# The first keys at the head of the DMA queue, with their last 2 KB columns in eight transfers of 8 rows

## The chip, the core and the metric

The kernel runs on one core of a Trainium2 chip. A core has five engines that run their own instruction streams and meet only at semaphores: TensorE (PE, matrix products; its weight loads are listed as PEld), VectorE (DVE), ScalarE (ACT), GpSimd (POOL) and SyncE (SP). Data come from HBM by DMA transfers. Here all of them are issued from SP's queue, one after the other, and carried by 16 DMA engines that work side by side. The metric is device time in microseconds, the median of several runs; a profiled execution gives the trace behind the views that are quoted.

## What is computed

One decode step, for four sequences of one token each, through two layers of the same weights: attention over a long cache of keys and values, then a gated feed-forward block, and both again.

```python
B, Sq, D = 4, 1, 512
Hq, Hkv, Sk, Dh = 32, 8, 8192, 128

def _A_ref(x, k_cache, v_cache, wq, wo):
    q = (x @ wq).reshape(B, Sq, Hq, Dh).transpose(0, 2, 1, 3)
    k = jnp.repeat(k_cache, rep, axis=1)
    v = jnp.repeat(v_cache, rep, axis=1)
    p = _softmax(jnp.einsum("bhqd,bhkd->bhqk", q, k) * (Dh ** -0.5))
    o = jnp.einsum("bhqk,bhkd->bhqd", p, v)
    return o.transpose(0, 2, 1, 3).reshape(B, Sq, Hq * Dh) @ wo

def _B_ref(x, w_gate, w_up, w_down):
    return (_silu(x @ w_gate) * (x @ w_up)) @ w_down

x = x + _A_ref(_layernorm(x), k_cache, v_cache, wq, wo)
x = x + _B_ref(_layernorm(x), w_gate, w_up, w_down)
x = x + _A_ref(_layernorm(x), k_cache, v_cache, wq, wo)
x = x + _B_ref(_layernorm(x), w_gate, w_up, w_down)
```

All inputs are bf16. The two caches are 67 MB each and both layers read both, so nearly all of the kernel's bytes are keys and values.

## The kernel before

**Tiles.** A unit `u` is one batch entry with a pair of key-value heads; there are 16 (`NP`). The keys of a unit are one tile of 128 rows by 32 KB (4 MB), and so are its values: row `p` holds 128 consecutive positions (`TT`) of one head, rows 0 to 63 the first head of the pair, rows 64 to 127 the second. Tiles lie in a ring of four slots of SBUF (`kv[:, s, :]`, `s` 0 to 3; a fifth slot, `QS`, holds `wq` at first). A slot is counted in eight parts (`NB`) of 4 KB columns (`BW` = 2048 elements); the set `free` and the resource names `s0.3` and so on go by such parts.

**What is done with a tile.** VectorE turns the keys in place, in blocks of 32 by 32 (`turn`, L484 with the instruction on L488): part by part for the first unit of a layer, two parts at once for most others. TensorE multiplies each part with the placed queries `zq` (`scores`, L505 with L512: four products of 128 x 512 per part). Then come the maximum, the exponentials (ScalarE, L559), the turned probabilities (L576) and the products with the values (L644). When a part of a tile is used up, `finished` calls `freed`, and that calls `pump`.

**What sets the order of the transfers.** The list `cmds` (L347 to L365) holds every load in the order in which SP issues it: the first keys `K(0, us[0])`, the second keys, the first values, then the other keys and values in turn, with the four pieces of `wo` inserted, the feed-forward weights behind them, and layer 1. A function per entry (`half`, `twos`, `ends`) cuts a tile into several transfers of fewer columns. `pump` (L406) issues entries from the front of the list for as long as the parts that they fill are free, and stops at the first that isn't. SP issues in that order and never out of it; a transfer whose slot is still being read waits on SP for the reader's semaphore, and everything behind it waits too. `load` (L425) issues one entry. A load of a whole tile counts on its slot's semaphore, a part of one on a semaphore of its own (`part_sem`).

**The start.** Lines L926 to L929 issue `wq`'s first half (2 MB), the token rows `A_x` (4 rows of 1 KB, into `xio`), `wq`'s second half, and then call `pump`, which issues keys 0, keys 1, values 0, `wo` piece 0 and keys 2; the next entry, values 1, needs slot 0 and stops it. TensorE transposes the token rows (L932), `center` (L807) takes the mean off, `qproj` (L834) makes the queries with `wq` (two passes of 64 products each, L841, the deviation in between, L827 to L831) and places them (L502). Only then does the loop over the units begin, with the turns of keys 0.

**The end.** The last transfers are layer 1's last values, the gate and up weights, and the down weights in three pieces (`wd0`, `wd1`, `wd2`; 608.21, 608.69 and 632.87 us). The last products (L903) wait for each piece in turn; their sums are copied (L965, L967) and stored.

Of the kernel before, what the change touches and what calls it, by code (L numbers as in the profile page):

```python
# [103 lines left out]
def bass_interleave_layers__gqa_block_cached__swiglu_ffn__decode_kernel(  # L104
# [18 lines left out]
    P = 128  # L123
# [6 lines left out]
    NB = 8  # L130
# [7 lines left out]
    QH = NB // NH  # L138
    assert 2 * QH * REP == QB and QH * Dh == 512
    ZP = QB - REP  # L140
    NSLOT = 4
# [3 lines left out]
    with ExitStack() as es:  # L145
        sb = lambda name, shape, dt: es.enter_context(nc.sbuf_tensor(name, shape, dt))

        SL = TT * Dh
        BW = TB * Dh
# [6 lines left out]
        kv = kvf[:, 0:(NSLOT + 1) * SL].rearrange("p (s w) -> p s w", s=NSLOT + 1)  # L156
# [63 lines left out]
        n = FO * B  # L220
# [8 lines left out]
        xio = pb[0:B, 0:D]  # L229
        acc2 = pbf[:, Dh:2 * Dh]  # L230
        row = acc2[0:B]
        PB = ["pb", "gr", "eg", "gw", "hT", "xs", "vs", "lnv", "xx", "xc", "row"]
# [39 lines left out]
        sem_x = sem("sem_x")  # L272
# [5 lines left out]
        def part_sem():  # L278
            n_part[0] += 1
            return sem(f"sem_p{n_part[0]}")  # L280

        es.enter_context(nc.Block())
        T = _Sync(engines, prog)
# [6 lines left out]
             reads=["ident"], writes=["ident"])  # L290
        T.op("pool", lambda e: e.memset(quad[:], 0.0), writes=["quad"])
        for a in range(NA):
# [11 lines left out]
             reads=["ident"], writes=["head"])  # L304
# [3 lines left out]
             reads=["ident"], writes=["made"])  # L308
        T.op("dve", lambda e: e.tensor_reduce(sel[:].rearrange("p (h r) -> p h r", h=2),
                                              made.rearrange("p (h q r) -> p h r q", h=2, q=QH), AX.X, ALU.max),  # L310
             reads=["made"], writes=["sel"])
        T.op("dve", lambda e: e.tensor_reduce(own[:], made.rearrange("p (h q r) -> p q h r", h=2, q=QH),
                                              AX.XY, ALU.max),
             reads=["made"], writes=["own"])
# [7 lines left out]
        order = [list(range(NP)), [NP - 1, NP - 2, NP - 3, NP - 4] + list(range(NP - 4))]  # L322
        turn_of = {}

        K = lambda L, u: ("K", L, u)
# [10 lines left out]
        ends = lambda it, s: [(it, s, 0, QH), (it, s, QH, NB - 1), (it, s, NB - 1, NB)]  # L336
# [3 lines left out]
        def placed(seq, ring, parts):  # L340
            out = []
            for i, it in enumerate(seq):
                s = ring[i % len(ring)]
                out += parts[i](it, s) if i in parts else [(it, s, 0, NB)]
            return out
# [1 line left out]
        us = order[0]  # L347
        seq = [K(0, us[0])] + loads(0, 1)
        assert len(seq) == 2 * NP
        cmds = placed(seq, (0, 1, 2, 3), {len(seq) - 1: ends})  # L350
        where = {it: s for it, s, _, _ in cmds}
        assert [where[it] for it in (K(0, NP - 1), V(0, NP - 2), V(0, NP - 1))] == [0, 2, 3]
        for n, i in ((3, 0), (6, 1), (9, 2), (12, 3)):
            cmds.insert(n, (("wo", i), None, 0, 0))
        cmds += [(("W", 0), W_SLOT[0], 0, NB), (("W+", 0), W_SLOT[0], NB, NB + 1)]

# [14 lines left out]
        def load_weight(name, i=0, s=0):  # L371
            if name == "wq":
                n = 2 * HqDh
                T.dma("sp", kv[:, QS, i * n:(i + 1) * n],
                      A_wq[i * 2 * P:(i + 1) * 2 * P, :].rearrange("(p e) f -> p (e f)", e=2), sem_w["wq"][i],
                      writes=[f"wq{i}"])
            elif name == "wo":
                src = A_wo[i * H2 * Dh:(i + 1) * H2 * Dh, :]
                T.dma("sp", wo_sb[:, i * H2:(i + 1) * H2, :].rearrange("p (c j) n -> p c (j n)", j=NA),
                      src.rearrange("(c p j) n -> p c (j n)", p=P, j=NA), sem_w["wo"][i], writes=[f"wo{i}"])  # L380
            else:
                w0 = kvf[:, s * SL:(s + 1) * SL]
                if name == "W+":
                    load_wd(w0, i, NW - 1, ["late"])
                    return
                T._wait("pool", T._need((), [f"s{s}.{NB - 1}"]))
                T.op("pool", lambda e: e.memset(late_pT(s).bitcast(FP32), 0.0), writes=["late"])
                T.dma("sp", w0[:, 0:KT * F].rearrange("p (c x) -> p c x", c=2),
                      B_w_gate.rearrange("(c p e) f -> p c (e f)", c=2, e=2), sem_w["wg"][0],
                      writes=[f"s{s}.{q}" for q in range(NB)] + ["wg"])  # L390
                up = B_w_up.rearrange("(c p e) f -> c p (e f)", c=2, e=2)
                if i == 0:
                    T.dma("sp", wres[:, 0:2 * F], up[0], sem_w["wu"][0], writes=["wu0"])
                    T.dma("sp", wres[:, 2 * F:], up[1, :, 0:FY], sem_w["wu"][1], writes=["wu1"])
                T.dma("sp", w0[:, O_WU:O_WD], up[1, :, FY:], sem_w["wu"][2], writes=["wu2"])

                for j in range(NW - 1):
                    load_wd(w0, i, j)
# [4 lines left out]
                  B_w_down[a * P:b * P, :].rearrange("(m p e) n -> p m (e n)", p=P, e=e_), sem_w["wd"][j],  # L403
                  writes=[f"wd{j}"] + list(also))

        def pump():  # L406
            while issued[0] < len(cmds):
                it, s, a, b = cmds[issued[0]]
                if it[0] == "wo":
                    load_weight(*it)  # L410
                else:
                    need = {(s, q) for q in range(a, b)}
                    if not need <= free:
                        return
                    free.difference_update(need)
                    if it[0] in ("W", "W+"):
                        load_weight(it[0], it[1], s)
                    else:
                        slot_of[it] = s
                        load(it, a, b, sem_s[s] if b - a == NB else part_sem())  # L420
                issued[0] += 1

        q_gone = set()

        def load(it, a, b, sm):  # L425
            kind, L, u = it
            s = slot_of[it]
            gp, bt = pair_gb(u)
            src = (A_k_cache if kind == "K" else A_v_cache)[bt, 2 * gp:2 * gp + 2, :, :].rearrange(
                "h (p t) d -> (h p) (t d)", t=TT)  # L430
            over = [w for i, w in enumerate(WQ) if s == QS and a // (NB // 2) == i and w not in q_gone]
            q_gone.update(over)
            T.dma("sp", kv[:, s, a * BW:b * BW], src[:, a * BW:b * BW], sm,
                  writes=[f"s{s}.{q}" for q in range(a, b)] + over)

        def freed(s, a, b):
            free.update((s, q) for q in range(a, b))
# [46 lines left out]
        def turn(L, u, q, n):  # L484
            s = slot_of[K(L, u)]
            w = kv[:, s, q * BW:(q + n) * BW].bitcast(FP32)
            names = [f"s{s}.{i}" for i in range(q, q + n)]
            T.op("dve", lambda e: e.transpose(w, w), reads=names, writes=names)  # L488
            turned.update((L, u, i) for i in range(q, q + n))
# [317 lines left out]
        def center(between=lambda: None):  # L807
            T.op("dve", lambda e: e.tensor_reduce(xs, xT[:].rearrange("p (k b) -> p b k", b=B), AX.X, ALU.add),
                 reads=["x"], writes=["xs", "pb", "row"])
            at, name = place("ln", 0, B)  # L810
            T.op("pe", lambda e: e.matmul(at, lhsT=ones, rhs=xs, start=True, stop=True),
                 reads=["xs", "onesf"], writes=[name])
            between()
            total = at.unsqueeze(1).to_broadcast([P, KT, B])
            T.op("dve", lambda e: e.scalar_tensor_tensor(bk3(xn[:]), total, -1.0 / D, bk3(xT[:]),
                                                         op0=ALU.mult, op1=ALU.add),
                 reads=["x", name], writes=["xn"])
            T.op("dve", lambda e: e.scalar_tensor_tensor(bk3(xc), total, -1.0 / D, bk3(xT[:]),
                                                         op0=ALU.mult, op1=ALU.add),
                 reads=["x", name], writes=["xc"])  # L820
            T.op("dve", lambda e: e.tensor_tensor(xx, xc, xc, ALU.mult), reads=["xc"], writes=["xx"])
            T.op("dve", lambda e: e.tensor_reduce(vs, xx.rearrange("p (k b) -> p b k", b=B), AX.X, ALU.add),
                 reads=["xx"], writes=["vs"])
# [99 lines left out]
            add_to_x(bank(k)[:, 0:XB], f"pb{k}")  # L923


        load_weight("wq", 0)  # L926
        T.dma("sp", xio, A_x.rearrange("b s d -> (b s) d"), sem_x, writes=PB)
        load_weight("wq", 1)
        pump()  # L929
        xb = bank_bf(OUTB)  # L930
        for kt in range(KT):
            T.op("pe", lambda e: e.matmul(xb[:, kt * B:(kt + 1) * B], lhsT=xio[:, pick2(kt)],  # L932
# [3 lines left out]
        for L in range(2):  # L936
            us = order[L]
            turn_of.update((u, i % 2) for i, u in enumerate(us))
            totals.clear()
            mixed.clear()  # L940
            center()
            qproj(L, us[0])
            if L:
                for q in (NB - 2, NB - 1):
                    hold(q, True)
                freed(QS, NB // 2, NB - 2)
            todo = [("K", 0)]
            for i in range(1, NP - 1):
                todo += [("K", i), ("V", i - 1)]
            todo[-1:] = [("K", NP - 1)] + [("V", i) for i in range(NP - 3, NP)]  # L950
            for kind, i in todo:
                if kind == "V":
                    values(L, us[i])
                    continue
                keys(L, us[i], us[min(i - 1, NP - 3)] if i else None, AHEAD if L and i == 1 else LAG)
            drain(0.0)
            flush()
            center(lambda: x_rows(0) if L else None)
            ffn(L)
# [39 lines left out]
```

## Time and profile before

| What | Value |
|---|---|
| Median of 3 runs | 647.24 us (647.04 to 647.56) |
| The profiled execution: its own time | 647.04 us |
| Its span, first to last recorded instruction | 645.2 us (1.8 us of its time lie outside) |
| Granted TensorE clock, mean | 0.83 |
| Busy: PE, PEld, DVE, ACT, POOL | 419.2, 181.6, 422.1, 41.2, 11.1 us |
| Bytes read from HBM | 272.9 MB, 423 GB/s over the span |
| First key turn of VectorE (L488) | 24.37 us |
| First product of scores (L512) | 25.67 us |
| Slot 0 free, values 1 issued by SP | 35.11 us |
| Output issued by SP | 643.61 us |

Busy times are sums over the span; an engine that is idle two fifths of the time in the mean can still be the one waited for in a stage. The clock of the profile runs in microseconds from the span's start, and "granted clock" is the share of full speed that TensorE was allowed.

Beside the instructions, the trace has a record for each DMA packet (start, duration, size, queue) and for each step of each DMA semaphore. A transfer of 128 rows raises its semaphore in 16 steps, one when each DMA engine has landed its share. The packets carry no engine's number, but each engine's packets follow one another without a gap, so that the time of the 16 steps shows how the engines stand against each other.

### The profile page before, as it was taken

The page shows a single profiled execution, that of the slowest core. Times are in us where ns is not written, and L with a number is a line of the kernel's source. Part 1 is how long each engine was busy: PE and PEld are TensorE (multiplying, and loading weights), DVE is VectorE, ACT ScalarE, POOL GpSimd, SP SyncE. Part 2 cuts the span into 40 slices and gives each one's busy share as a digit, 9 for nine tenths or more (in the row PEclk, how much of TensorE's full clock was granted, in tenths as well). Part 3 has the DMA queues.
Part 4 walks back from the last instruction along what each step waited for, and adds up shares of the span by engine and source line. Part 5 has one row for each costly group of instructions (what it writes and reads, how often), then busy time and mean ns, then how long its engine had stood idle before and what let it go on. Part 6 is the DMA issues. An engine that isn't in the chain of part 4 may idle for free.

```text
span 645.2 us, 7417 instructions
## 1 busy us (share of the span) xinstructions
PE 419.2 (65%) x3128; PEld 181.6 (28%) x3128; DVE 422.1 (65%) x595; ACT 41.2 (6%) x117; POOL 11.1 (2%) x43
## 2 busy tenths in 40 slices
PE   3483475456765756757867877777555676557877
PEld 2121122122222312322226432233222222222325
DVE  1585467456776556776962778878655577665964
ACT  1000000000000000000010010000000000000110
POOL 0000000000000000000000000000000000000000
PEclk9995887688876888777975899997768987679787
DMA  9999999999999999999999999999999999999997
GB/s 366 442 425 416 441 430 431 424 429 438 433 425 432 439 424 430 431 439 426 427 414 410 421 440 430 427 432 434 427 428 439 428 431 427 440 427 428 433 416 276
DMA packets 14560, 273.36 MB, mean 424 GB/s; under 512 B 1464, under 2 KB 1472, under 8 KB 5312
## 3 DMA queue, kind: packets, MB, share of 16 engines
q1 hardware_dynamic: 14528, 272.91, 99.2%
q8 instruction: 24, 0.39, 0.2%
q14 instruction: 8, 0.07, 0.0%
HBM read 272.90 MB, written 0.00 MB: 423 GB/s over the span
## 4 chain that ended last, share of the span: by engine, by line
DMA 62%; DVE 20%; PE 13%; issue 3%; another core or an unknown queue 1%; SPq 0%; ACTq 0%; ACT 0%; DVEq 0%
DMA kvf<-in_A_k_cache_dram 50%; DVE kvf L488 16%; DMA kvf<-in_A_v_cache_dram 11%; PE ps L512 8%; PE ps L644 2%; DMA kvf<-in_B_w_down_dram 2%; DVE pb L694 1%; PE ps L841 1%; PE ps L882 0%; DVE pb L690 0%; DVE kvf L453 0%; DVE scr L704 0%; SPq L93 0%; PE ps L523 0%
## 5 line engine op out<-in xcount | busy, mean ns | idle before, releaser
L512 PE MATMUL ps<-kvf,zq 128*128 128x512 bf16 x1024 | 296.1, 436 | 191.9 <-DVE kvf L488 188.2
L488 DVE STREAM_TRANSPOSE kvf<-kvf 128x2048 f32<-128x2048 f32 (+1 forms) x135 | 280.3, 2102 | 127.9 <-DMA kvf<-in_A_k_cache_dram 127.8
L512 PEld LDWEIGHTS ps<-kvf,zq 128*128 128x128 bf16 x1024 | 100.3, 109 | 349.9 <-DVE kvf L488 230.2
L644 PE MATMUL ps<-kvf,pT 128*32 128x512 bf16 x960 | 65.8, 396 | 1.4 <-DVE pT L576 1.4
L559 ACT ACTIVATE pb<-ps,tiny 128x512 bf16<-128x512 f32 x32 | 22.0, 688 | 537.3 <-DVE tiny L557 500.7
L576 DVE STREAM_TRANSPOSE pT<-pb 64x512 bf16<-64x512 bf16 x60 | 41.2, 687 | 3.6 <-ACT pb L559 2.6
L694 DVE SCALAR_TENSOR_TENSOR pb<-ps,tiny,pb 128x128 f32<-128x128 f32 x104 | 36.5, 351 | 4.4 <-PE ps L644 0.7
L518 DVE TENSOR_REDUCE tiny<-ps 128x1 f32<-128x512 f32 x32 | 22.0, 687 | 21.4 <-PE ps L512 21.4
L644 PEld LDWEIGHTS ps<-kvf,pT 128*32 128x32 bf16 x960 | 20.8, 98 | 31.0 <-issue 15.3
L699 PEld LDWEIGHTS ps<-sel,pb 128*128 128x128 f32 x64 | 16.8, 271 | 16.4 <-DVE pb L694 7.9
L502 POOL TENSOR_TENSOR zq<-scr,tiny 128x64 bf16<-128x64 bf16 x30 | 9.0, 299 | 563.3 <-PE ps L512 563.3
L526 DVE TENSOR_REDUCE mrm<-ps 1x8 f32<-1x128 f32 x32 | 8.8, 274 | 13.8 <-PE ps L523 13.8
L549 PEld LDWEIGHTS ps<-mrm,tiny 128*128 128x128 f32 x60 | 13.4, 229 | 9.4 <-DVE scr L704 3.2
L699 PE MATMUL ps<-sel,pb 128*128 128x8 f32 x64 | 12.4, 267 | 5.3 <-DVE pb L694 5.3
L549 PE MATMUL ps<-mrm,tiny 128*128 128x16 f32 x60 | 10.2, 248 | 3.1 <-ACT mrm L561 3.1
L690 DVE TENSOR_SCALAR pb<-ps,tiny 128x128 f32<-128x128 f32 x32 | 10.1, 316 | 2.6 <-PE ps L644 2.6
L760 PE MATMUL ps<-wo_sb,scr 128*4 128x512 bf16 x48 | 11.0, 379 | 0.6 <-DVE scr L729 0.6
L523 PE MATMUL ps<-identf,tiny 128*1 128x128 f32 x32 | 8.6, 270 | 1.8 <-DVE tiny L518 1.8
L561 ACT ACTIVATE mrm<-head,tiny 128x8 f32<-128x8 f32 x32 | 9.6, 300 | 1.0
L841 PE MATMUL ps<-xn,kvf 128*128 128x4 bf16 x256 | 7.4, 166 | 1.9 <-DMA kvf<-in_A_wq_dram 1.1
L882 PE MATMUL ps<-xn,kvf 128*128 128x4 bf16 x224 | 7.2, 169 | 1.6 <-DMA kvf<-in_B_w_up_dram 1.2
L841 PEld LDWEIGHTS ps<-xn,kvf 128*128 128x128 bf16 x256 | 7.3, 105 | 2.1 <-DMA kvf<-in_A_wq_dram 1.2
(83 smaller groups left out, 113.7 us busy)
## 6 DMA issues: line engine op xcount, KB each, us to landing
kvf<-in_A_k_cache_dram SPq DMA_DIRECT2D x28, 4096.0 KB, 31.0
kvf<-in_A_v_cache_dram SPq DMA_DIRECT2D x27, 4096.0 KB, 35.2
kvf<-in_A_v_cache_dram SPq DMA_DIRECT2D x4, 2048.0 KB, 18.4
kvf<-in_A_k_cache_dram SPq DMA_DIRECT2D x7, 1024.0 KB, 9.8
kvf<-in_A_wq_dram SPq DMA_DIRECT2D x2, 2048.0 KB, 10.1
wo_sb<-in_A_wo_dram SPq DMA_DIRECT2D x4, 1024.0 KB, 41.3
kvf<-in_B_w_gate_dram SPq DMA_DIRECT2D x2, 1792.0 KB, 23.6
kvf<-in_A_v_cache_dram SPq DMA_DIRECT2D x2, 1536.0 KB, 34.1
```

Of the source, the lines that this page charges most:

```text
L488: T.op("dve", lambda e: e.transpose(w, w), reads=names, writes=names)
L512: T.op("pe", lambda e: e.matmul(bank(bk)[:, 0:SW], lhsT=zq[:, z0:z0 + P], rhs=w[:, :, c // 2, :, c % 2], start=(q == 0 and c == 0), stop=( ...
L518: T.op("dve", lambda e: e.tensor_reduce(mx[:], bank(bk)[:, 0:SW], AX.X, ALU.max), reads=[f"pb{bk}"], writes=["mx"])
L549: T.op("pe", lambda e: e.matmul(at, lhsT=ones, rhs=mrm[:, i * H2:(i + 2) * H2], start=True, stop=True), reads=[f"m8{i}", "rsm", "onesf"], ...
L559: T.op("act", lambda e: e.activation(pb[:], bank(bk)[:, 0:SW], ACTF.Exp, bias=nm, accum_out=rs), reads=[f"pb{bk}", "nm"], writes=PB + ["rs"])
L576: T.op("dve", lambda e: e.transpose(dst, pb[hp]), reads=["pb", "row"], writes=[name])
L644: T.op("pe", lambda e: e.matmul(bank(k)[j * QB:(j + 1) * QB, q0 * Dh:q1 * Dh], lhsT=p_t[:, t, h, :], rhs=v[:, q0:q1, t, :], start=((last o ...
L690: T.op("dve", lambda e: e.tensor_scalar(into, o, own[:, q:q + 1], None, op0=ALU.mult), reads=[f"pb{k}", "own"], writes=["row"] if last els ...
L694: T.op("dve", lambda e: e.scalar_tensor_tensor(into, o, own[:, q:q + 1], into, op0=ALU.mult, op1=ALU.add), reads=[f"pb{k}", "own", iname], ...
L699: T.op("pe", lambda e: e.matmul(at, lhsT=into, rhs=sel[:], start=True, stop=True), reads=[iname, "sel"], writes=[name])
L760: T.op("pe", lambda e: e.matmul(bank(OUTB)[0:B, 0:D], lhsT=oT[:, h, :], rhs=wo_sb[:, h, :], start=(gp == groups[L][0] and r == 0), stop=(g ...
L841: T.op("pe", lambda e: e.matmul(at[:, h * B:(h + 1) * B], lhsT=wq_sb[:, kt, h * Dh:(h + 1) * Dh], rhs=xn[:, kt * B:(kt + 1) * B], start=(k ...
```

## The change

```diff
-        cmds = placed(seq, (0, 1, 2, 3), {len(seq) - 1: ends})
+        cmds = placed(seq, (0, 1, 2, 3), {0: half, len(seq) - 1: ends})
...
-        for n, i in ((3, 0), (6, 1), (9, 2), (12, 3)):
+        for n, i in ((4, 0), (7, 1), (10, 2), (13, 3)):
...
-        def pump():
-            while issued[0] < len(cmds):
+        def pump(most=len(cmds)):
+            while issued[0] < most:
...
+        LOW, H, BESIDE = BW // 2, P // 2, NSLOT - 1
+        low_unit = K(0, order[0][0])
+
+        def raised():
+            s, c = slot_of[low_unit], SL - LOW
+            U16 = mybir.dt.uint16
+            T.op("dve", lambda e: e.tensor_copy(kv[H:P, s, c:SL].bitcast(U16), kv[0:H, BESIDE, c:SL].bitcast(U16)),
+                 reads=["low"], writes=[f"s{s}.{NB - 1}", f"s{BESIDE}.{NB - 1}"])
...
-            T.dma("sp", kv[:, s, a * BW:b * BW], src[:, a * BW:b * BW], sm,
-                  writes=[f"s{s}.{q}" for q in range(a, b)] + over)
+            names = [f"s{s}.{q}" for q in range(a, b)]
+            c = b * BW - LOW if (it, b) == (low_unit, NB) else b * BW
+            T.dma("sp", kv[:, s, a * BW:c], src[:, a * BW:c], sm, writes=names + over)
+            if c < b * BW:
+                both = src[:, c:SL].rearrange("(h p) w -> p h w", h=2)
+                sm = part_sem()
+                for j in range(NB):
+                    T.dma("sp", kv[j:H:NB, s:BESIDE + 1:BESIDE - s, c:SL], both[j:H:NB], sm,
+                          writes=["low"] if j == NB - 1 else [])
...
+        pump(1)
+        T.dma("sp", xio, A_x.rearrange("b s d -> (b s) d"), sem_x, writes=PB)
+        pump(2)
         load_weight("wq", 0)
-        T.dma("sp", xio, A_x.rearrange("b s d -> (b s) d"), sem_x, writes=PB)
         load_weight("wq", 1)
-        pump()
+        pump(5)
...
             center()
+            if not L:
+                for q in range(0, NB, 2):
+                    if q == QH:
+                        raised()
+                        pump()
+                    turn(L, us[0], q, 2)
             qproj(L, us[0])
```

In SP's queue the order is now: the first half of keys 0 (128 rows by 16 KB), the token rows, the second half without its last 2 KB (128 by 14 KB), eight small transfers, `wq` in two halves, keys 1, values 0 and `wo` piece 0. Each small transfer `j` takes the last 2 KB of rows j, j+8, ... j+56 of both heads: 8 partitions by two places by 2 KB, 32 KB in all. The first head's rows land where they belong in slot 0, the second head's land in partitions 0 to 63 of slot 3, which is still empty. `raised` copies these from slot 3 to partitions 64 to 127 of slot 0, and keys 2, which go to slot 3, wait on SP for that copy. The four turns of keys 0, two parts each, now stand on VectorE ahead of `qproj`, with the copy between the second and the third; TensorE's order of products is as before.

## The prediction

> **What bounds the kernel now.** I first read the slices of the span and the DMA queues on the profile's page.
>
> ```profile
> DMA  9999999999999999999999999999999999999997
> GB/s 366 442 425 416 441 430 431 424 429 438 433 425 432 439 424 430 431 439 426 427 414 410 421 440 430 427 432 434 427 428 439 428 431 427 440 427 428 433 416 276
> ...
> q1 hardware_dynamic: 14528, 272.91, 99.2%
> q8 instruction: 24, 0.39, 0.2%
> q14 instruction: 8, 0.07, 0.0%
> ```
>
> The 16 DMA engines work from the first slice to the last but one. The time is theirs, unless a stage hides a pause. The table of windows asks that stage by stage (columns: stretch and its length, busy us and instructions of PE, PEld, DVE, ACT, POOL, then clock, DMA share, GB/s):
>
> ```profile
> 2.00:17.00 15.00, 5.40 (x152) 4.92 (x152) 2.37 (x12) 0.58 (x3) 0.10 (x1) 1.00 0.97 406
> 17.00:50.00 33.00, 19.67 (x100) 7.28 (x100) 21.18 (x21) 1.08 (x3) 0.60 (x2) 1.00 1.00 428
> 50.00:300.00 250.00, 150.48 (x888) 60.23 (x888) 158.76 (x198) 14.02 (x40) 3.59 (x12) 0.79 1.01 431
> ```
>
> No pause: the share stays at 1, while PE and DVE work 150 and 159 of 250 us. The chain of waits and the totals of waits seem to say otherwise:
>
> ```profile
> DMA kvf<-in_A_k_cache_dram 50%; DVE kvf L488 16%; DMA kvf<-in_A_v_cache_dram 11%; PE ps L512 8%; PE ps L644 2%; DMA kvf<-in_B_w_down_dram 2%; DVE pb L694 1%; PE ps L841 1%; PE ps L882 0%; DVE pb L690 0%; DVE kvf L453 0%; DVE scr L704 0%; SPq L93 0%; PE ps L523 0%
> ...
> DVE kvf L488 <- DMA kvf<-in_A_k_cache_dram: 127.8, 24, 8.8
> ```
>
> The chain walks from a turn back to the issue of its keys and from there to the product that freed the slot, so turns get 16%. But a key tile lands 31.0 us after its issue (median on the page) and takes 9.7 to carry: some 20 us of it is queueing behind earlier tiles. DVE waits for the DMA, not the reverse. The end, in the timeline:
>
> ```profile
> 641.12 1.80 PE L903 MATMUL ps<-kvf,pb 128*4 128x128 bf16 x56
> 642.53 0.10 PEld L903 LDWEIGHTS ps<-kvf,pb 128*4 128x4 bf16 x8 [0.25 <-DMA kvf<-in_B_w_down_dram]
> 642.94 0.59 DVE L967 CAST pb<-ps 4x128 bf16<-4x128 f32 x2 [1.88 <-PE ps L903]
> 643.61 0.29 SPq L969 DMA_DIRECT2D out_dram<-pb  x1
> ```
>
> The last products wait for the last piece of the down weights; 2.7 us later (645.2 - 642.49) all is over. So the question is what sets 642.49, and the answer is in the trace's semaphore records. For three transfers: when the first of the 16 DMA engines had landed its share, and how much later the others had (us).
>
> ```
> keys 0          22.50  0.00 0.05 0.07 0.09 0.10 0.12 0.13 0.14 0.16 0.21 0.22 0.23 0.41 0.51 0.90 1.85
> values, L0     285.28  0.00 0.03 0.04 0.13 0.38 0.47 0.90 1.55 1.56 1.59 1.61 1.62 1.63 1.70 1.82 2.13
> down, piece 2  638.31  0.00 0.06 0.14 0.38 0.54 0.76 0.81 2.51 3.66 3.69 3.71 3.79 3.86 3.89 3.96 4.18
> ```
>
> DMA engines fall behind one at a time, in jumps of about 1.45. The packet records show why: at 18.81 the first of the 24 instruction packets of 16 KB (q8) sits in one engine's stream and takes 1.0 us, and the key packet behind it takes some 0.45 longer than its neighbours; 48.95, 87.47, 128.17 repeat it. 24 packets on 8 engines are 3 each, 4.3 us; at the end eight engines are 2.5 to 4.2 behind and eight within 0.81. The second eight carry no such packets, have idled a little between the layers (about 352 to 362 us), and wait for nobody. **The end is that of the eight late DMA engines, which never pause.**
>
> **The change part by part.**
>
> *Bytes between DMA engines.* A transfer of 128 rows gives each engine 8 rows. The token load of 4 rows shows in the packets as one 1 KB row on each of four engines, none on the other twelve. By that row I take an 8-row transfer to use eight engines, the same eight in all eight transfers. The other eight lose 8 rows x 2 KB. A key tile advances an engine by 9.715 us (landings, 275.57 to 285.28) for 8 rows of 32 KB, so 2 KB are 0.0759 and the eight rows 0.607. Keys 0 now also come in two pieces; a halved tile advances 4.90 per half (618.13 to 623.03), not 4.86: +0.045 for one more transfer. Lighter eight: 0.045 - 0.607 = **-0.56**. Heavier eight: 16 packets of 2 KB, 0.080 from start to start in the last down weights, 1.28, plus 0.006 to 0.045 for each of eight transfers, less 0.607, plus 0.045: +0.77 to +1.08, and I take +0.9.
>
> [...]
>
> *Which eight are late?* The engine hit at 18.81 is none of the four that carried the tokens (followed packet by packet from 7.5 us). Later hits can't be told apart, since streams then coincide within 1 ns. If the token engines belong to the eight that get the small transfers, this speaks for the late ones being the other eight. I take that: -0.56 at the end.
>
> *SP.* Nine more issues at about 0.4 us (0.38 and 0.36 in the timeline) make some 4 us. They lie beside 10 us of queued keys. Without that cover they would cost 4 us.
>
> *wq, moved behind keys 0.* In before `wq` has landed at 13.68; now 4 MB later, about 23.4 to 24.5. From its landing to placed queries is 3.0 us (13.68 to 16.68): first products at 26.4 to 27.5, not 25.67. The turns, 4 x 2.30 = 9.2 for 8 x 1.14, then lie between 11 and 20, when DVE idled 7.4 us; the copy (64 rows of 1024 16-bit elements) between 0.4 (the 128x256 cast) and 0.7 (the 64x512 transpose), taken as 0.7, fits there too. Then 32 products at 0.24 (8 in 1.91 us) or at the mean row's 0.436 are 7.6 to 14 us: slot 0 free at 34.0 to 41.5, not 35.11. Values 1 are issued up to 6 us later, but keys 2 keep the queue busy to 54.2. The second keys, freed at 45.9, slip to 52 at most, with work queued to 66. PE catches up after 50 (150 of 250 us). Cost 0; it would cost only beyond some 13 us.
>
> *The new wait on SP.* Keys 2 wait for the copy, near 15 to 17 us; behind them stand values 1 and all else. DMA has `wq`, keys 1, values 0 and `wo` until 44.5 us. Cost 0; without that cover, the delay of the copy.
>
> *The tail* follows the last landing unchanged. Sum, against the profiled execution: span 645.2 - 0.56 = 644.6, its time 647.04 - 0.56 = 646.5. The median lies 0.2 above that execution, 647.24, which gives **646.7 us**.
>
> **Rivals.**
>
> *The heavier eight are the late ones.* Then the end moves by +0.77 to +1.08: 648.0 to 648.3. For it: only one hit could be placed. Against: that one.
>
> *Each small transfer costs its whole landing.* The output store of 4 KB, alone in the queue, lands 1.27 us after its issue (643.61 to 644.88). If eight in a row each held their engines so long, 10.2 us replace 0.61; less the 3.4 by which the latest of the eight leads at the end and the 0.65 of pause it could skip, 5.5 us remain: 652.8, slower. It decides from 0.58 us a transfer. Against: consecutive transfers in the queue add 0.045, and landing is paid beside the next ones. [...]
>
> *The early keys bring the pipeline forward.* If the chain of waits were the bound, the end would follow slot 0: at best from 35.11 to 34.0, -1.1, and -0.56 more from the relieved engines: -1.7, 645.6, faster by 0.26%. For it: the chain. Against: queueing of 20 us behind every issue.
>
> *It does nothing that shows.* If the small transfers spread over all 16 engines, only the cost of more packets stays: +0.05 to +0.3, 647.3 to 647.5. Against: the token load's four packets.
>
> **How the numbers follow.** Forecast 0.60; early keys 0.15; no shift 0.10; heavier eight late 0.10; whole landings 0.05. About 0.2% (1.3 us) is what a measurement of this kernel can tell from no change. The forecast is -0.09%: within. Of its 0.60 and the rivals near zero, 0.66 stay within; faster 0.21 (the early keys and fetches that fall better than here); slower 0.13 (whole landings, and a heavier eight that pays more than the row of 0.080 says). The forecast's own range is 646.2 to 647.0; the range with the cases that are left, 645.5 to 648.3.
>
> **What would show it.** The landings of keys 0 should have two groups, eight engines about 1.4 us behind the other eight; at the last down weights eight engines should still be last, by some 2 us instead of 3.6, and the last step should come near 641.9. First turns near 11 us, first products near 27, values 1 issued between 34 and 41.5, and DMA at 1.00 in the windows to 300 us. Wrong if the last step comes later than 642.5, if the eight small transfers take over 4.6 us on their engines, or if the DMA share drops before 60 us.

## The result: 648.64 us, 1.45 us slower

| | Median | Range | Runs |
|---|---|---|---|
| Before, in the same measurements | 647.19 us | 646.86 to 647.56 | 11 |
| With the change | 648.64 us | 648.36 to 649.69 | 11 |

The ratio is 1.0023, with a 95% interval of [1.0015, 1.0031]: slower. The middle of the interval lies a little above the 0.2% that the prediction took for the least that can be told here, its lower end a little below. The time is outside the predicted range of 646.2 to 647.0, and outside 645.5 to 648.3, the range with the other cases. The profiled execution took 648.36 us, its span 646.6 us; before it was 647.04 and 645.2.

**The slices and the queues of the changed kernel** look much as before:

```profile
DMA  8999999999999999999999999999999999999996
GB/s 342 448 426 417 425 443 430 422 427 443 426 422 443 430 423 435 438 424 431 436 406 410 421 433 435 436 423 429 442 421 432 435 430 432 429 434 429 430 415 262
...
q8 instruction: 24, 0.39, 0.2%
q14 instruction: 8, 0.07, 0.0%
```

No slice shows a pause. **The windows of the changed kernel** (columns as before: PE, PEld, DVE, ACT, POOL busy, then clock, DMA share, GB/s) do show something:

```profile
12.00:14.00 2.00, 0.00 (x0) 0.00 (x0) 2.00 (x2) 0.00 (x0) 0.00 (x0) 1.00 1.12 294
14.00:17.00 3.00, 0.00 (x0) 0.00 (x0) 2.73 (x3) 0.00 (x0) 0.00 (x0) 1.00 1.00 426
17.00:22.00 5.00, 2.30 (x66) 2.21 (x66) 2.74 (x2) 0.19 (x1) 0.00 (x0) 1.00 0.99 423
22.00:50.00 28.00, 21.87 (x180) 9.33 (x180) 13.01 (x15) 1.45 (x5) 0.60 (x2) 1.00 1.01 430
50.00:300.00 250.00, 150.19 (x888) 60.20 (x888) 157.62 (x198) 14.03 (x40) 3.59 (x12) 0.80 1.00 430
```

From 12 to 14 us, while the eight small transfers are carried, the DMA engines are recorded as busy all the time and move 294 GB/s instead of some 430. The busy share of 1.12 shows nothing of it; the last column does. Over two microseconds this column scatters: the same stretch reads 557 in the kernel before, and 401 and 483 in the first two kernels of the experiments, in which nothing is held up. 294 lies below all of these, and the durations of the packets, further down, are the firmer evidence. The stretches after it move 423 to 430 GB/s.

**The timeline of the start**, changed kernel (start, duration, engine, line, operation):

```profile
1.61 5.55 SPq L93 DMA_DIRECT2D kvf<-in_A_k_cache_dram  x9
7.20 0.92 SPq L93 DMA_DIRECT2D kvf<-in_A_wq_dram  x2
...
10.04 4.49 DVE L504 STREAM_TRANSPOSE kvf<-kvf 128x2048 f32<-128x2048 f32 x2
14.78 0.42 DVE L431 COPY kvf<-kvf 64x1024 uint16<-64x1024 uint16 x1 [0.24 <-DMA kvf<-in_A_k_cache_dram]
15.23 0.34 SPq L93 DMA_DIRECT2D kvf<-in_A_k_cache_dram  x1
15.23 4.50 DVE L504 STREAM_TRANSPOSE kvf<-kvf 128x2048 f32<-128x2048 f32 x2
...
27.40 3.17 PE L528 MATMUL ps<-kvf,zq 128*128 128x512 bf16 x7 [0.35 <-DVE zq L518]
```

The reordered work does what the forecast said: `wq` is issued while 7 us of queued transfers are still being carried, the turns begin at 10.04, the copy takes 0.42 and releases keys 2 on SP at once, the scores begin at 27.40. Values 1 are issued at 36.77 (35.11 before), keys 3 at 46.33 (45.90): the pipeline has caught up.

**The timeline of the end**, changed kernel:

```profile
642.51 1.80 PE L919 MATMUL ps<-kvf,pb 128*4 128x128 bf16 x56
643.92 0.10 PEld L919 LDWEIGHTS ps<-kvf,pb 128*4 128x4 bf16 x8 [0.26 <-DMA kvf<-in_B_w_down_dram]
644.34 0.60 DVE L991 CAST pb<-ps 4x128 bf16<-4x128 f32 x2 [1.88 <-PE ps L919]
645.01 0.30 SPq L993 DMA_DIRECT2D out_dram<-pb  x1
```

The weights wait for the last down weights as before, only later: their last step came at 643.88 instead of 642.49, +1.39, and the 2.7 us behind it are the same. The loss is all in the landings. Here are the semaphore steps of the changed kernel in the form of the prediction's table (first engine, and how much later the others):

```
keys 0, second half     11.97  0.00 0.03 0.05 0.07 0.12 0.13 0.18 0.23 0.24 0.31 0.32 0.33 0.34 0.34 0.36 0.59
wq, first half          17.86  0.00 0.02 0.04 0.09 0.14 0.14 0.15 0.17 1.29 1.31 1.31 1.48 1.49 1.51 1.57 1.57
down, piece 2, layer 0 347.63  0.00 0.01 1.11 1.31 1.43 1.45 1.51 1.59 1.84 1.89 2.69 2.85 2.91 2.92 3.07 4.22
down, piece 2, layer 1 639.24  0.00 0.12 0.15 0.53 0.57 0.80 1.18 1.73 2.96 2.97 3.03 3.12 3.14 4.33 4.45 4.64
```

The two groups of eight are there after the small transfers. But half of `wq` advances an engine by 4.90, and the lighter eight took 17.86 - 11.97 = 5.89: they were late by 0.99, where they should have been on time. The packet records say why. The 2 KB packets take 0.084 us until 12.0, then up to 0.178 (mean of all 128: 0.116). `wq`'s 16 KB packets on the other engines take 0.95 to 1.05 us between 12 and 13.5, and 0.611 to 0.626 from 14.5 on.

### The profile page after: what moved, and what is told of

It is laid out like the page before. It is cut to its first block, busy times and chain, and to the rows that moved or that the text cites. A ratio compares the mean times of both kernels' runs of the same rounds, so it can differ in the third digit from the quotient of the medians.

```text
span 646.6 us, 7422 instructions
## 1 busy us (share of the span) xinstructions
PE 414.7 (64%) x3126; PEld 179.1 (28%) x3128; DVE 422.0 (65%) x592; ACT 41.2 (6%) x117; POOL 11.1 (2%) x43
## 4 chain that ended last, share of the span: by engine, by line
DMA 60%; DVE 20%; PE 14%; issue 3%; SPq 1%; ACT 0%; ACTq 0%; DVEq 0%
DMA kvf<-in_A_k_cache_dram 45%; DVE kvf L504 16%; DMA kvf<-in_A_v_cache_dram 11%; PE ps L528 9%; DMA kvf<-in_A_wq_dram 3%; DMA kvf<-in_B_w_down_dram 2%; PE ps L660 2%; DVE pb L710 2%; SPq L93 1%; PE ps L857 1%; DVE pb L706 0%; PE ps L898 0%; DVE ps L472 0%; DVE kvf L469 0%; PE ps L539 0%
## 5 line engine op out<-in xcount | busy, mean ns | idle before, releaser
L528 PE MATMUL ps<-kvf,zq 128*128 128x512 bf16 x1024 | 292.6, 431 | 185.8 <-DVE kvf L504 180.8
L528 PEld LDWEIGHTS ps<-kvf,zq 128*128 128x128 bf16 x1024 | 99.0, 108 | 342.8 <-DVE kvf L504 225.1
L715 PEld LDWEIGHTS ps<-sel,pb 128*128 128x128 f32 x64 | 16.5, 266 | 16.0 <-DVE pb L710 7.8
```

What stands on the lines that cost most here:

```text
L528: T.op("pe", lambda e: e.matmul(bank(bk)[:, 0:SW], lhsT=zq[:, z0:z0 + P], rhs=w[:, :, c // 2, :, c % 2], start=(q == 0 and c == 0), stop=( ...
L715: T.op("pe", lambda e: e.matmul(at, lhsT=into, rhs=sel[:], start=True, stop=True), reads=[iname, "sel"], writes=[name])
```

## The experiments

The edits are against the changed kernel, those of the two ladders against the kernel before; `...` marks lines left out. "Latest" is the last of 16 steps of a transfer.

### The order alone, and one transfer in place of eight

```diff
-            c = b * BW - LOW if (it, b) == (low_unit, NB) else b * BW
+            c = b * BW
...
-                        raised()
```

> Keys 0 go first in two whole halves (128 rows by 16 KB), their turns stand ahead of the queries, and there are no small transfers and no copy. Theory A (the loss is made by the eight small transfers: they weigh on DMA engines that turn out to be late, and slow the others while they run): 646.9 to 647.3, no change; wq's first half lands 4.9 us after keys 0's second half on every DMA engine, and at wq's second half the 16 steps lie as before, within 0.9 of each other, not in two groups. Rival B (the new order itself costs, by a later start of the products or the wait of later loads): 648.2 to 648.7, with the small transfers adding nothing.

Measured: 647.01 us, ratio 0.9998 [0.9989, 1.0007]. `wq`'s first half comes 4.90 behind keys 0 on all 16 engines. From 12 us on (windows of the kernel with the order alone):

```profile
12.00:14.00 2.00, 0.00 (x0) 0.00 (x0) 2.00 (x2) 0.00 (x0) 0.00 (x0) 1.00 0.94 401
14.00:17.00 3.00, 0.00 (x0) 0.00 (x0) 3.00 (x3) 0.00 (x0) 0.00 (x0) 1.00 1.02 437
```

The early keys, the early turns and the late `wq` cost nothing and bring nothing that the interval of 0.1% to either side could show. This kernel is the base of the comparisons below.

```diff
-                for j in range(NB):
-                    T.dma("sp", kv[j:H:NB, s:BESIDE + 1:BESIDE - s, c:SL], both[j:H:NB], sm,
-                          writes=["low"] if j == NB - 1 else [])
+                T.dma("sp", kv[:, s, c:SL], src[:, c:SL], part_sem(), writes=["low"])
```

> The last 2 KB columns of keys 0 come by one transfer of 128 rows instead of eight of 8 rows, with no copy; order as in the changed kernel. Theory A (uneven load): every DMA engine carries 8 packets of 2 KB, no two groups; if only the uneven load and not the 2 KB pieces are at fault, packets of 0.08 to 0.09 us and 647.0 to 647.4. Theory C (2 KB reads 32 KB apart crowd the same part of memory, whoever makes them): packets of 0.15 us or more, every engine 0.5 to 0.8 later at wq's first half, and 647.7 to 648.1 in the end.

```profile
12.00:14.00 2.00, 0.00 (x0) 0.00 (x0) 2.00 (x2) 0.00 (x0) 0.00 (x0) 1.00 1.15 483
```

Measured: 647.01 us, ratio 0.9995 [0.9986, 1.0004]. All 128 packets of 2 KB took 0.084, `wq`'s beside them 0.611. (In place of the copy, VectorE waits for the transfer.) Packets of 2 KB are not the cause.

### Is it where the eight transfers read?

Their rows lie 256 KB apart in HBM (8 rows of 32 KB). Here each reads 32 KB that lie together, so that the last 8 positions of each row of keys 0 are other data.

```diff
-                    T.dma("sp", kv[j:H:NB, s:BESIDE + 1:BESIDE - s, c:SL], both[j:H:NB], sm,
+                    T.dma("sp", kv[j:H:NB, s:BESIDE + 1:BESIDE - s, c:SL],
+                          src[j].rearrange("(p h w) -> p h w", p=NB, h=2), sm,
```

> The eight small transfers keep their shape and destination but each reads one stretch of 32 KB without gaps, so the last 2 KB columns of the first keys hold other data. Theory C (rows 256 KB apart slow the memory): packets of 2 KB back at 0.08 us, wq's 16 KB packets beside them at 0.61, wq's first half 4.9 us behind keys 0 on the eight lighter engines, heavier ones still 1.3 to 1.5 behind these; end 0.5 to 0.9 earlier than the changed kernel, 647.7 to 648.1, still slower than before, since heavier engines are among the late ones. Rival D (eight engines with small packets slow the rest whatever they read): packets at 0.16, 5.9 us, and 648.6 as in the changed kernel.

```profile
12.00:14.00 2.00, 0.00 (x0) 0.00 (x0) 2.00 (x2) 0.00 (x0) 0.00 (x0) 1.00 1.15 303
```

Measured: 648.74 us, ratio 1.0025 [1.0016, 1.0035], as the changed kernel; 2 KB packets up to 0.179, `wq`'s 0.94 to 1.05. It isn't the reads.

### A ladder of transfers, first a failed marking

Meant to mark the DMA engines by giving each another load: transfers of 1, 2, ... 15 neighbouring rows of 4 KB behind keys 0 of the kernel before, with all of `wo` moved ahead of values 0.

```diff
+        for r in range(1, NA * KT):
+            s, o = 2 + (r - 1) // 8, (r - 1) % 8 * BW
+            T.dma("sp", kv[0:r, s, o:o + BW], src[0:r, o:o + BW], sm,
```

> The kernel before with fifteen extra transfers of 1, 2, ... 15 rows by 4 KB behind keys 0 (unused data into slots 2 and 3) and all of wo ahead of values 0, so that each DMA engine lags by a different amount, about 0.16 us a step and 2.4 us in all. It is a marking, not an improvement. Each later instruction packet moves one engine by 1.45 us, and its place in the order tells which. The prediction's assumption: all packets hit the eight engines that a transfer of 8 rows leaves out. Theory A: two or more of the engines hit are among the eight that it uses.

Measured: 654.61 us in a single execution. As a mark it is useless, since it holds up everything. Windows of this kernel:

```profile
22.00:25.00 3.00, 0.00 (x0) 0.00 (x0) 0.00 (x0) 0.00 (x0) 0.00 (x0) 1.00 1.47 194
25.00:30.00 5.00, 0.17 (x1) 0.13 (x2) 1.47 (x2) 0.00 (x0) 0.00 (x0) 1.00 0.86 133
```

DMA "busy" at 0.86 to 1.47 and 133 to 194 GB/s. 4 KB packets took 0.605 instead of 0.159 (the first ones), and 32 KB packets beside them 4.4 instead of 1.213. 0.605 / 0.159 is 3.8. The rows of a transfer are neighbours here, 0 to 14 at most, and my guess was that the partitions which they are written to make the difference. The ladder with rows 4 apart (8 KB, 1 to 8 rows) agrees:

```diff
+            T.dma("sp", kv[0:4 * r - 3:4, s, o:o + 2 * BW], src[0:4 * r - 3:4, o:o + 2 * BW], sm,
```

> The kernel before with eight extra transfers of 1, 2, ... 8 rows by 8 KB behind keys 0, rows 4 apart (unused data into slots 2 and 3), and all of wo ahead of values 0. [...] Theory A: two or more of the eight stepped engines are hit. The prediction's assumption: none is.

```profile
22.00:25.00 3.00, 0.00 (x0) 0.00 (x0) 0.55 (x1) 0.00 (x0) 0.00 (x0) 1.00 1.09 467
```

Measured: 648.28 us in a single execution; from 22 us on every 8 KB packet took 0.309, and the 32 KB packets beside them 1.213 to 1.218. Nothing is held up. Which engines are hit by instruction packets could not be followed from it for sure, since streams with lags within 0.1 us can't be told apart; I read from it that none of the strongly loaded engines is hit, and that reading was wrong (below).

### The eight transfers with rows 4 apart

In the change the eight rows of a small transfer are 8 apart (0, 8, ... 56); in the ladder whose packets kept their 0.309 and 1.213 they are 4 apart. If the distance is what matters, the small transfers with rows 4 apart should have the 0.084 and 0.611 of the one transfer.

```diff
-                    T.dma("sp", kv[j:H:NB, s:BESIDE + 1:BESIDE - s, c:SL], both[j:H:NB], sm,
+                    o = j // NA * QB + j % NA
+                    rows_ = slice(o, o + 4 * NB - 3, 4)
+                    T.dma("sp", kv[rows_, s:BESIDE + 1:BESIDE - s, c:SL], both[rows_], sm,
```

> The eight small transfers keep size and data, but each takes rows 4 apart (o, o+4, ... o+28, for o = 0 to 3 and 32 to 35) in place of rows 8 apart, so that no two of the eight DMA engines write into partitions of the same group of four modulo 32. [...] Rival D (eight engines with small packets slow the rest in any case): 648.6, packets at 0.16.

```profile
12.00:14.00 2.00, 0.00 (x0) 0.00 (x0) 2.00 (x2) 0.00 (x0) 0.00 (x0) 1.00 1.06 435
14.00:17.00 3.00, 0.00 (x0) 0.00 (x0) 2.94 (x3) 0.00 (x0) 0.00 (x0) 1.00 1.02 437
```

Measured: 647.72 us, ratio 1.0009 [1.0000, 1.0018]. The same eight transfers, bytes and engines; the windows have 435 GB/s in place of 294, the 2 KB packets their 0.084 (all but four, which took up to 0.138) and the 16 KB packets 0.611. Of the change's 1.63 us over the base (648.64 - 647.01), 0.92 is gone, and 0.71 stays. Each of these two steps is smaller than the intervals are wide, and neighbouring intervals overlap; but the last step of the last down weights, in the profiled executions, moves by the same amounts, 643.88 to 642.98 and 642.98 to 642.28. What stays is left for the uneven load. The same with 4 KB columns doubles it:

```diff
-        LOW, H, BESIDE = BW // 2, P // 2, NSLOT - 1
+        LOW, H, BESIDE = BW, P // 2, NSLOT - 1
```

> [...] If late engines are among the eight that carry more, the end moves by another 0.6 to 0.7 (16 packets of 4 KB at 0.16 for 16 of 2 KB at 0.084, less 8 x 0.076): 648.2 to 648.7. If the late engines were all among the others, as predicted, it would fall by another 0.6, to 647.0 or less.

Measured: 648.50 us, ratio 1.0020 [1.0011, 1.0029], 1.49 over the base: twice 0.71, and with an interval clear of the base's. (Of it, the last step of the down weights shows 643.50 - 642.28 = 1.22 in the profiled execution, whose end lies 3.7 behind that step where the others have 2.7 to 3.2; why is open.)

### Can fewer engines carry it?

Four rows to a transfer put the whole load on four DMA engines (their landings, below, stand 2.60 to 2.63 behind the first), and twelve are relieved. In the expectations the lower eight are the engines that carry transfers of 8 rows, the upper eight the others, and the first four those that carry transfers of 4 rows; no record numbers them. I expected a gain, since I took the first four for engines that no instruction packet hits.

```diff
+            for j in range(2 * NB):
+                o = j // 4 * 16 + j % 4
+                rows_ = slice(o, o + 13, 4)
+                T.dma("sp", kv[rows_, s:BESIDE + 1:BESIDE - s, c:SL], both[rows_], sm,
...
         load_weight("wq", 0)
+        tail()
         load_weight("wq", 1)
```

> The last 2 KB columns come by sixteen transfers of 4 rows (rows 4 apart, so that the four writers stay out of each other's partitions), queued behind wq's first half. The whole load of these columns then lies on four DMA engines, and twelve lose 0.61 us. Theory (the late engines of the end are the upper eight and one or two of the lower eight, but none of the first four, since the run with transfers of 1 to 8 rows showed no fetch on a strongly loaded engine): twelve engines 0.56 earlier, four some 1.9 later, which still end ahead of the late ones; 647.0 - 0.56 = 646.4 to 646.6, last step of the last down weights near 641.8 to 642.1. Rival, one of the first four engines is among the late ones: 647.0 + 1.9 = 648.5 to 649.0. Rival, the end follows the sum of the bytes over all engines and not the latest one: 647.0.

> The same with the last 3 KB columns: twelve DMA engines lose 0.91 us, four carry about 2.9 more. Theory: 647.0 - 0.86 = 646.1 to 646.3, 0.3 below the run with 2 KB. Rival, a late engine among the first four: 649.5 to 650. Rival, the sum of the bytes decides: 647.0.

Measured: 650.22 us, ratio 1.0047 [1.0035, 1.0060], and with 3 KB columns (`LOW = 3 * BW // 4`) 652.09 us, 1.0081 [1.0067, 1.0095]: the gain didn't come, and both are beyond even the rival's times. The rival's mechanism, a late engine among the first four, is there, but two things come together. First, 2 KB packets are held up again, to 0.288 (next section), although the rows of each transfer are 4 apart. Second, the landings show one of the four loaded engines being delayed further, each time at one of the eight q14 packets (8 KB, so far left out of account). The four latest offsets of five transfers of the first of these kernels:

```
first landing     four latest offsets
        54.80     2.60 2.61 2.62 2.63
        86.48     2.61 2.63 2.66 3.63    q14 packet at  83.8
       227.65     2.53 2.54 2.56 4.49    q14 packet at 225.9
       333.56     3.01 3.07 3.21 4.31
       334.83     3.01 3.07 3.22 5.26    q14 packet at 338.3
```

(A late engine carries its share of a transfer later, so that the packet at 338.3 falls into a share that lands at 334.83 + 5.26. From 333 us on engines hit by q8 packets have passed two of the four loaded ones, which then stand at 2.31 and 2.34.) One of the four DMA engines that a transfer of 4 rows uses is set back by some 0.95 each time. Of the other three none moves when one of the first eight q8 packets comes: at 276.21 they still stand at 2.51, 2.52 and 2.55.

### Whose partitions?

Each of the four engines has eight 2 KB packets in each of the four groups of rows, 0 to 15, 16 to 31, 32 to 47 and 48 to 63. Their packets took 0.084 from 16.5 to 17.5 us, up to 0.288 until 18.5, 0.084 to 0.132 until 19.25, and 0.15 to 0.18 in the median after that: fast, slow, fast, slow. Counted packet by packet, a slow stretch begins some four packets of each engine after the first row of its group, so the assignment to rows is a reading and not a measurement. By that reading it isn't only the transfer's own rows that must lie apart: these four engines are fast in partitions 0 to 15 and 32 to 47, and slow in the others. The theory, A in the second of the two expectations below, became: what counts is whether other engines write to the same partitions at that time, and those in which an engine is fast are its own. It is a guess: no packet record names an engine or a partition. Two runs try it by the durations: the eight rows 4 apart moved to partitions 64 to 127, and four rows to a transfer in partitions 0 to 15 and 32 to 47 alone.

Against the kernel with rows 4 apart, and with the copy turned round:

```diff
-            T.op("dve", lambda e: e.tensor_copy(kv[H:P, s, c:SL].bitcast(U16), kv[0:H, BESIDE, c:SL].bitcast(U16)),
+            T.op("dve", lambda e: e.tensor_copy(kv[0:H, s, c:SL].bitcast(U16), kv[H:P, BESIDE, c:SL].bitcast(U16)),
...
-                    T.dma("sp", kv[rows_, s:BESIDE + 1:BESIDE - s, c:SL], both[rows_], sm,
+                    T.dma("sp", kv[H + o:H + o + 4 * NB - 3:4, s:BESIDE + 1:BESIDE - s, c:SL], both[rows_], sm,
```

> As the run with rows 4 apart, but the eight rows land in partitions 64 to 127 (the first head's columns stay there and the second head's are copied down, so the two heads have their last 8 positions of each row exchanged). The eight writers are again in eight different groups of four partitions. [...] Theory B (only the small transfer's own rows must lie in different groups): as with rows 4 apart, 0.084 and 0.611, 647.7.

```profile
12.00:14.00 2.00, 0.00 (x0) 0.00 (x0) 2.00 (x2) 0.00 (x0) 0.00 (x0) 1.00 1.22 279
14.00:17.00 3.00, 0.00 (x0) 0.00 (x0) 2.33 (x3) 0.00 (x0) 0.00 (x0) 1.00 0.91 372
```

Measured: 649.08 us, ratio 1.0031 [1.0018, 1.0044]: 279 GB/s, 2 KB packets from 12.25 us on with a median of 0.168, `wq`'s of 1.12 to 1.19 between 12.2 and 13.6, `wq`'s first half 6.15 behind keys 0. Theory B is refuted: against rows 4 apart in partitions 0 to 63, the same rows read, the packets alone leave no doubt (0.168 against 0.084), and the times agree (649.08 against 647.72). Where the rows are written makes the difference; in partitions 64 to 127 rows 4 apart didn't help.

The other run, as an edit of the kernel with four rows to a transfer:

```diff
-            T.op("dve", lambda e: e.tensor_copy(kv[H:P, s, c:SL].bitcast(U16), kv[0:H, BESIDE, c:SL].bitcast(U16)),
+            T.op("dve", lambda e: e.tensor_copy(kv[:, s, c:SL].bitcast(U16), kv[:, s, c - LOW:c].bitcast(U16)),
...
-                T.dma("sp", kv[rows_, s:BESIDE + 1:BESIDE - s, c:SL], both[rows_], sm,
+                f = j % 8 // 4 * 32 + j % 4
+                T.dma("sp", kv[f:f + 13:4, BESIDE, j // 8 * BW:(j // 8 + 1) * BW].rearrange("p (h w) -> p h w", h=2),
+                      both[rows_], sm,
```

> As the run with sixteen transfers of 4 rows, but all of them land in partitions 0 to 15 and 32 to 47 of the empty slot and are not used; VectorE fills the last 2 KB columns of keys 0 with the 2 KB ahead of them, so that 16 of 128 positions in each row are repeated. The bytes of each DMA engine are the same as there. Theory A: the four engines write to their own partitions only; no packet is held up (0.084 and 0.611), wq's second half is 4.9 less 0 us behind the first on twelve engines and 2.6 later on four, 1.33 us less than in the run with sixteen transfers: median 650.2 - 1.3 = 648.9 if one of the four is among the late engines at the end (the landings of that run speak for it), 646.4 to 646.6 if none is. Theory B (sixteen transfers in a row, or four engines with twice the packets, cost by themselves): 650.2.

Windows of the kernel with four rows to a transfer in partitions 0 to 63, and of the one with 0 to 15 and 32 to 47 alone:

```profile
17.00:20.00 3.00, 2.29 (x66) 2.21 (x66) 0.00 (x0) 0.36 (x2) 0.00 (x0) 1.00 1.08 306
```

```profile
17.00:20.00 3.00, 2.29 (x66) 2.21 (x66) 0.00 (x0) 0.30 (x2) 0.00 (x0) 1.00 1.00 412
```

The 2 KB packets are back at 0.084 (all but six, between 17.5 and 17.9 us, which took 0.125 to 0.292), the 16 KB packets from 18 us on all at 0.611 (between 16.4 and 17 us, as the four turn to the small rows, ten took 0.68 to 1.07; both stay unexplained), and `wq`'s second half lands at 21.82 on the relieved engines instead of 23.09. The packets agree with theory A. The time is 649.71 us (1.0037 [1.0024, 1.0050]), which lies between theory A's 648.9 and theory B's 650.2 and overlaps the interval of four rows in partitions 0 to 63, so the time alone would not decide: only 0.5 of the 1.27 comes through to the end. One engine, with the steps of the q14 packets, is the latest at the end of layer 0 (5.65 behind the first) and of layer 1 (5.15). It is 1.04 earlier than in the other kernel at the end of layer 0 (353.32 to 352.28), but only 0.36 at the third landing after these weights (360.72 to 360.36), and 0.31 at the end (645.27 to 644.96). So most of the gain was lost between the layers; why is open.

### What carries a lag to the end

One table over all profiled executions: the latest engine at the last down weights of each layer, the distance, and the median time (of the two ladders, the single execution).

```
                               layer 0   layer 1   between   median
before                          350.66    642.49    291.83   647.24
order alone                     350.68    642.28    291.60   647.01
one transfer                    350.50    642.29    291.78   647.01
rows 4 apart                    351.27    642.98    291.71   647.72
the same, 4 KB                  351.36    643.50    292.14   648.50
the change                      351.86    643.88    292.03   648.64
contiguous reads                351.93    643.94    292.00   648.74
rows 4 apart, 64 to 127         352.19    644.31    292.13   649.08
four rows, 0-15 and 32-47       352.28    644.96    292.68   649.71
four rows                       353.32    645.27    291.95   650.22
four rows, 3 KB                 355.10    647.23    292.13   652.09
ladder, neighbouring rows       357.95    649.93    291.98   654.61
ladder, rows 4 apart            351.60    643.64    292.04   648.28
```

Whatever was done at 12 us, the end is the latest DMA engine of layer 0 plus 291.6 to 292.7. No run got a relieved engine's gain to the end.

## Why the prediction was wrong

- **The order, SP's issues, the turns, the copy, the new wait: right, at no cost.** The nine issues on SP took 5.55 us, not 4, the copy 0.42, first products at 27.40 (forecast 26.4 to 27.5), values 1 at 36.77 (34.0 to 41.5). The order alone is 0.9998 of before.
- **Eight engines lighter, eight heavier: right.** Two groups of eight appear. With rows 4 apart the lighter eight are 0.59 ahead of the base at `wq` (16.91 against 17.50; forecast 0.56) and still at the end of layer 0 (346.52 against 347.11). The heavier eight are 0.62 behind (18.54 against 17.92), less than the forecast 0.77 to 1.08.
- **"Heavier eight: 16 packets of 2 KB, 0.080 from start to start": failed.** The row came from a transfer of 128 rows. In eight rows 8 apart a packet took up to 0.178 and 0.116 in the mean, where one transfer of 128 rows has 0.084 throughout and rows 4 apart have it for all but four packets, and the heavier eight are 1.51 behind the base (19.43 against 17.92), 0.89 more than with rows 4 apart.
- **"Lighter eight: 0.045 - 0.607 = -0.56": failed in the change.** The sum took the lighter eight as undisturbed by the small transfers. Their `wq` packets of 12 to 13.5 us went from 0.611 to some 0.96, and they came out +0.36 behind the base (17.86 against 17.50) instead of 0.59 ahead. With rows 4 apart the excess of both terms is gone, worth 0.9 us at the end.
- **"I take that: -0.56 at the end" (which eight are late): failed, and would have made the rest wrong too.** The sum gave the late engines the 24 instruction packets of q8 alone, and the eight of q14 stood unused in the first fence. One engine, one of the four that a transfer of 4 rows uses, takes q14 packets at some 0.95 each: in the changed kernel the last of the heavier group goes from 1.54 behind to 2.36 at 86, 3.33 at 227 and 4.23 at 334 us, and is the latest at the end of layer 0. Of the first eight q8 packets of the changed kernel, six move an engine of the lighter eight back (of these, four are left within 0.13 of each other at 207.88, and two at 266.21), and those at 160 and 199 us move one of the others, from 1.3 to 1.5 behind the first to 2.93 and 2.77. The kernel with rows 4 apart shows six and two as well. So the guess was right for six of the eight engines that q8 hits, if these are eight different ones, as the kernel before suggests; but two of them and the q14 engine belong to the heavier group, and one late engine there is enough. Uneven load costs 0.7 with the packets at 0.084 and 0.611 (rows 4 apart).
- **"Eight engines are 2.5 to 4.2 behind and eight within 0.81": misread.** The row has nine and seven, and so has the row of the values (nine at 1.55 or more). Eight hits of q8 don't make nine late engines. In the kernel before, one engine goes from some 0.2 behind to 1.18 at the q14 packet of 63.6 us and from 1.15 to 2.12 at that of 207.0: it is the 2.13 at the end of the second row. The sign of the missing term stood in the prediction's own table.
- **"The end is that of the late DMA engines, which never pause": right in the main**, by the table above: layer 0's latest engine sets the end to within 1.1 us over all runs, and to within 0.54 without the run with four rows in partitions 0 to 15 and 32 to 47, which lost something between the layers. The tail of 2.7 us was right.
- **The rivals.** That the heavier eight are the late ones named the right sign, and 648.0 to 648.3 came within 0.4 by luck: it left the held-up packets out, and without them, with rows 4 apart, the late heavier eight make 647.72. The early keys as a gain, and whole landings at 1.27 each, are refuted by the order alone and by 0.084 packets.

What the prediction lacked is a look at which rows a small transfer writes. The packets of these runs took 3.8 times as long in neighbouring rows (0.605 against 0.159), up to 2.1 times in rows 8 apart (0.178 against 0.084), 2.0 times in eight rows 4 apart in partitions 64 to 127 (0.168) and 1.0 times in eight rows 4 apart in partitions 0 to 63. What makes them slow there is not shown.

**What stays open.** Why the packets of full transfers beside the small ones are held up as well (0.96 instead of 0.611 in the change; beside the ladder of neighbouring rows 32 KB packets took 4.4 instead of 1.213) is not shown; the runs only show that it comes with the slow small packets and vanishes with them. That engines have partitions of their own is my guess; the runs show the durations. Which engine each q8 packet hits was not settled, only the groups that the first eight hit. A version that relieves the late engines was not found: it would have to load only engines that neither q8 nor q14 hits, with packets that keep their 0.084, and with 2 KB columns the most that could be gained is the forecast's 0.56 us, an estimate, and little enough to be lost in the intervals. Nothing tried was faster than before.

## What to carry to other kernels

In these runs a transfer of few rows was paid by all engines when its packets were slow, and that followed from the rows that it wrote: 2 KB packets took up to 0.178 us in rows 8 apart (648.64 us) and 0.168 in the median in eight rows 4 apart in partitions 64 to 127 (649.08), but 0.084 in eight rows 4 apart in partitions 0 to 63 (647.72) and in one transfer of 128 rows, which cost nothing here (647.01). So try other rows before the bytes are blamed, or use 128 rows. The 16 DMA engines run without a pause here (a share of 1.00 from 50 to 300 us), and bytes taken from eight or twelve of them were worth nothing, since the latest one was not among them; find that one first, in every queue of the profile, small instruction queues too. And read GB/s beside the busy share: held-up packets counted as busy (1.12 at 294 GB/s).

## What the runs showed of the hardware

- 2 KB packets took 0.084 us in one transfer of 128 rows and, all but four (up to 0.138), in transfers of eight rows 4 apart in partitions 0 to 63. In rows 8 apart they took up to 0.178 (0.116 in the mean), in eight rows 4 apart in partitions 64 to 127 a median of 0.168. In four rows 4 apart they took up to 0.288 over partitions 0 to 63, and 0.084 (all but six, up to 0.292) in 0 to 15 and 32 to 47 alone. 4 KB packets in neighbouring rows took 0.605, the first ones 0.159.
- Packets of full transfers beside the slow ones slowed too: 16 KB from 0.611 to 0.95 to 1.05 us in the change, 32 KB from 1.213 to 4.4 beside the ladder of neighbouring rows.
- In the kernel before, an 8 KB q14 packet, recorded at some 0.33 us, set its engine back by 0.95 or a little more (from some 0.2 behind to 1.18, from 1.15 to 2.12); a 16 KB q8 packet, recorded at some 1.07, by 1.45.
- In the change, eight small transfers of two places took 0.63 us each to issue on SP (5.55 for them and one more), a whole tile 0.43.
